# Building the identity tiles on VectorE instead of GpSimd, and taking two buffers of the last block together, in a linear-attention, PReLU and soft-MoE kernel

## The chip, the cores and the metric

The kernel runs on one core of a Trainium2 chip. The metric is the device time of one execution in microseconds (us), as the median of several runs; a profile of one further execution tells where the time goes.

## The reference, cut to what matters

```
q, k, v: 8 batches x 8 heads x 576 x 64; w_phi: 64 x 128
phi(x): p = x @ w_phi; p = p - max|p| over the features; [exp(p), exp(-p)]
kv = phi(k)^T v;  z = sum over s of phi(k)
x  = (phi(q) kv) / (phi(q) . z + 1e-6)              -> 4608 x 512
h  = x @ w_in;  g = max(h, 0) + alpha * min(h, 0);  x = g @ w_out
logits = x @ phi (32 slots);  d = softmax over tokens;  slot_in = d^T x
slot_out = max(slot_in @ w1[e], 0) @ w2[e]           (8 experts, 4 slots each)
out = softmax over slots of logits, @ slot_out       -> 4608 x 512
```

All inputs are float32.

## The kernel before

The 4608 tokens are cut into 12 blocks of 384 columns. For each block the kernel forms the query features and attends (`q_pair`, four head pairs), divides (`q_finish`), multiplies by `w_in` in 16 chunks of 128 rows (`gemm`, 12 matmuls each, into the tile `ph`), applies the PReLU (`leaky`, tile `gT`), and turns each chunk into the tile `gb` by 32x32 block transposes (`turn_g`). `softmax` then takes the logits of a block, and its `gather` (line 596, tile `pS`) sums `gb` weighted by the exponentials. The key side (`k_pair`) is done along the way. `w_in` and `w_out` come in as 32-bit words of another float format and are turned into float32 by a chain of VectorE and ScalarE operations (`conv`, lines 187 to 199).

The query features need the largest absolute value of the projection over all 128 partitions. That is GpSimd's `partition_all_reduce` (line 405: `pj` in, `mb` out), 48 times in the program. VectorE subtracts it (line 409), and ScalarE takes the exponentials (line 415). GpSimd also clears small tiles `zt` with memsets (line 347). Line 126 (`make_identity`) builds the 128x128 identity `ident` on GpSimd: a memset (masks.py:197) and an affine select (masks.py:199). `ident` serves TensorE's transposes, and from it `setup_b` adds up `tident`, four 32x32 identities side by side, repeated down the partitions.

The program is written as steps of a list ("slots", sixteen to a block), and a scheduler then orders the instructions of each engine. Each engine runs its own instructions strictly in that order; transfers are issued by SyncE's queue, also in order.

`gb` has three buffers of 8 chunks. A block takes one at its chunk 0 and a second at its chunk 8, and gives them back when its gather has read them. When the last block is reached, buffers that have become free are filled with the weights of the experts (`fetch`, line 702): two pieces of 256 KB into each `w` buffer whose chunk has been multiplied (line 745), and six pieces into a `gb` buffer at slot 186 (line 747). At the end the kernel multiplies the slots by `w1` (line 805, tile `pe`) and `w2` (line 823, `pso`), forms the output (line 859, `po`), and writes it (line 867).

Of the kernel before, what the change touches and what calls it, by code (L numbers as in the profile page):

```python
# [9 lines left out]
F32 = mybir.dt.float32  # L10
# [4 lines left out]
ALU = mybir.AluOpType  # L15
# [11 lines left out]
BT = 384  # L27
NB = T // BT
# [35 lines left out]
def attention_prelu_softmoe(ctx: ExitStack, tc, qT, kT, v, wphi, w_in, w_out, alpha, phi, w1, w2, out):  # L64
    nc = tc.nc
# [14 lines left out]
    pools = {}  # L80

    def open_pool(name, side=None):
        cm = tc.tile_pool(name=name, bufs=1, side=side) if side else tc.tile_pool(name=name, bufs=1)
        pools[name] = cm, cm.__enter__()
        return pools[name][1]

    def close_pool(name):
        pools.pop(name)[0].__exit__(None, None, None)
# [3 lines left out]
    def together(calls, before=None):  # L92
        held = before is not None
        for i, call in enumerate(calls):
            if i == 0:
                ins = call().ins
            else:
                with tc.high_priority():
                    ins = call().ins
            if i or held:  # L100
                tc.add_manual_dep(ins, before.name, nosync, reason="issued together")
            before = ins
        return before

    def spin(count, before, turn=None):
        turn = turn or bank("spin", ps_d)
        return together([
            lambda i=i: nc.tensor.matmul(turn[:, 128 * (i % 4):128 * (i % 4) + 128], ident, ident, start=True, stop=True)  # L108
            for i in range(count)], before)

    def bank(name, pool=None):
        if pool is not None:
            return pool.tile([128, 512], F32, tag={id(ps_h): "h", id(ps_l): "l", id(ps_d): "d"}[id(pool)], name=name)
        return ps_a.tile([128, 512], F32, tag="a", name=name)
# [6 lines left out]
    prep = open_pool("prep")  # L121
# [1 line left out]
    att = open_pool("attq", "right")  # L123

    ident = const.tile([128, 128], F32, name="ident")
    make_identity(nc, ident)
    wp = att.tile([128, F], F32, name="wp")
    nc.sync.dma_start(wp, wphi)
    alpha_sb = const.tile([128, NC], F32, name="alpha_sb")
# [3 lines left out]
    tident = const.tile([128, 128], F32, name="tident")  # L133
# [7 lines left out]
    cm = const.tile([128, NT], F32, name="cm")  # L141

    def setup_a():
        nc.vector.memset(ones, 1.0)

    def setup_b():
        nc.sync.dma_start(alpha_sb, alpha)
        nc.vector.tensor_scalar(out=alpha_neg, in0=alpha_sb, scalar1=-1.0, scalar2=None, op0=ALU.mult)
        nc.sync.dma_start(phi_sb, phi.rearrange("(k p) s -> p k s", p=128))
        for j in range(4):  # L150
            o = tident[:, 32 * j:32 * j + 32]
            nc.vector.tensor_tensor(out=o, in0=ident[:, 0:32], in1=ident[:, 32:64], op=ALU.add)
            nc.vector.tensor_tensor(out=o, in0=o, in1=ident[:, 64:96], op=ALU.add)
            nc.vector.tensor_tensor(out=o, in0=o, in1=ident[:, 96:128], op=ALU.add)

    sched = {}
    mark = {}
# [3 lines left out]
    def step_of(slot):  # L161
        return slot + VS * sum(slot > r for r in after)
# [320 lines left out]
    gb, pl_t, gT_t = {}, {}, {}  # L483

    def gemm(n, c):
        xhi, xlo = xhi_t[n], xlo_t[n]
        ph = ps_h.tile([128, 512], F32, tag="h", name="ph")
        h = ph[:, 0:BT]
        first = [(k, a, b) for k in range(KD) for a, b in ((0, 0), (1, 0))] + [(k, 0, 1) for k in range(KD)]
        terms = first if c == 0 else [(k, a, b) for k in range(KD) for a, b in ((0, 0), (0, 1), (1, 0))]  # L490
        for i, (k, a, b) in enumerate(terms):
            gemm_last[0] = nc.tensor.matmul(  # L492
                h, (w_in_hi, w_in_lo)[a][c][:, 128 * k:128 * k + 128], (xhi, xlo)[b][:, k, :],
                start=(i == 0), stop=(i == len(terms) - 1)).ins
        return h

    def leaky(n, c, h):
        gT = gT_t[n, c] = sm.tile([128, 512], F32, tag="gT", name="gT", bufs=5)[:, 0:BT]
        if n < NDEF or (c % 2 == 0 and n < NB - 1):
            nc.scalar.activation(gT, h, AF.Relu, scale=-1.0)  # L500
            nc.scalar.activation(h, h, AF.Relu)  # L501
            ins = nc.vector.scalar_tensor_tensor(out=gT, in0=gT, scalar=alpha_neg[:, c:c + 1], in1=h, op0=ALU.mult, op1=ALU.add).ins  # L502
        else:
            nc.vector.tensor_scalar(out=gT, in0=h, scalar1=0.0, scalar2=alpha_sb[:, c:c + 1], op0=ALU.min, op1=ALU.mult)  # L504
            ins = nc.vector.scalar_tensor_tensor(out=gT, in0=h, scalar=0.0, in1=gT, op0=ALU.max, op1=ALU.add).ins
        mark[NC * n + c] = ins
        if n < NDEF:
            nc.sync.dma_start(gT_d[n, c], gT)
# [11 lines left out]

    def turn_g(n, c):
        gT = gT_t[n, c]
        if c % 8 == 0:
            gb[n, c // 8] = pools["gp"][1].tile([128, 8, BT], F32, tag="gb", name="gb", bufs=3)
        nc.vector.transpose(out=gb[n, c // 8][:, c % 8, :], in_=gT)  # L525
        if c % 4 == 3:
            if c == 3:
                pl_t[n] = (bank("pl") if n < NDEF else bank("pl", ps_l))[:, 0:BT]
            before = None
            if (n, c) == (NB - 1, NC - 1):  # L530
                before = spin(SPIN[0], gemm_last[0])
            last = together([
                lambda g=g: nc.tensor.matmul(  # L533
                    pl_t[n][32 * g:32 * g + 32, :], wpr[:, c - 3 + g, :], gT_t.pop((n, c - 3 + g)), start=(c == 3), stop=(c == NC - 1))
                for g in (3, 2, 1, 0)], before)
            if before is not None:
                spun[0] = spin(SPIN[1], last)
# [137 lines left out]
    at(NC * (NB - 1) - 6, "post", lambda: combine(0, NT - 8))  # L675
    at(NC * (NB - 1) + 8, "post", lambda: combine(NT - 8, NT - 4))
    at(-44, "pre", setup_a)
    at(-42, "pre", setup_b)

    pieces = [("wo", c) for c in range(NC)]  # L680
# [25 lines left out]
    for step in range(-45, step_of(nslots + 4)):  # L706
        slot = real.get(step)
        for fn in sched.get((step, "pre"), ()):
            fn()
        h = None  # L710
        if slot is not None:
            n, c = divmod(slot, NC)
            if 0 <= slot < nslots:
                h = gemm(n, c)
            pn, pc = divmod(slot - 1, NC)
            if NDEF <= pn < NB:
                turn_g(pn, pc)
        for fn in sched.get((step, "virtual"), []) + sched.get((step, "pe"), []) + sched.get((step, "pe2"), []):
            fn()
        if h is not None:  # L720
            leaky(n, c, h)
        for fn in sched.get((step, "post"), ()):
            fn()
        if slot is None:
            continue
        if slot == NC * NDEF:
            close_pool("prep")
            open_pool("gp")
        if slot == 152:
            for tag in ("kraw", "khi", "klo", "vte", "vto", "kp1", "ks"):  # L730
                fetch(attk, tag)
            for i in range(3):
                fetch(attk, "vg", 1, 3)
            for i in range(KPB):
                fetch(attk, "kp2", 2, KPB)
        if slot == 168:
            close_pool("attq")
            pf = open_pool("pf", "right")
            for i in range(PF):
                fetch(pf, f"pf{i}")  # L740
        if slot == NC * (NB - 1):
            fetch(xp, "num", 3)
            fetch(xp, "bc", 3)
        if NC * (NB - 1) < slot <= nslots:
            fetch(wring, f"w{(slot - 1) % NC}", 2)
        if slot == 186:
            fetch(pools["gp"][1], "gb", 6, 3)
        if slot == nslots:
            fetch(xp, "xhi", 3)
            fetch(xp, "xlo", 3)  # L750
    gp = pools["gp"][1]
# [40 lines left out]
    for eg in range(2):  # L792
        for j in range(4):
            nc.vector.tensor_reduce(
                out=own[:, j:j + 1], in_=ident[:, 36 * j + 16 * eg:36 * j + 16 * eg + 4], axis=AX.X, op=ALU.add)
# [3 lines left out]
    for eg in range(2):  # L799
        hr = attk.tile([128, EF], F32, tag="kp2", name="hr", bufs=KPB)  # L800
        for fh in range(2):
            pe = ps_h.tile([128, 512], F32, tag="h", name="pe")
            for k in range(KD):
# [3 lines left out]
                out=hr[:, 512 * fh:512 * fh + 512], in0=pe, scalar1=0.0, scalar2=own[:, 4 + eg:5 + eg], op0=ALU.max, op1=ALU.min)  # L807
        t = acc[2 * eg:2 * eg + 2]
        for b in range(2):
            nc.vector.transpose(  # L810
                out=t[b].rearrange("p (b s) -> p b s", s=32),
                in_=hr.rearrange("p (f b) -> p b f", b=32)[:, 16 * b:16 * b + 16])
# [110 lines left out]
```

## Time and profile before

| | us |
|---|---|
| median of 3 runs (lowest to highest) | 1011.63 (1010.61 to 1012.14) |
| profiled execution, its own time | 1010.69 |
| its span | 1008.9 |
| TensorE matmuls busy | 949.4 |
| VectorE busy | 761.1 |
| ScalarE busy | 446.1 |
| GpSimd busy | 145.1 |

Busy time counts instructions that work; register, branch, semaphore and DMA-issuing instructions do not count. TensorE is busy 94% of the span as a whole, but not everywhere: the first 25 us hold 8.7 us of matmuls. In the rows the engines are PE (TensorE), PEld (its weight loads), DVE (VectorE), ACT (ScalarE), POOL (GpSimd) and SP (SyncE); a q behind the name is the engine's instruction queue. A row of a timeline has the start and the duration in us, and in brackets the idle time of the engine just before and what ended it.

### The profile page before, as it was taken

The page shows a single profiled execution, that of the slowest core. Times are in us where ns is not written, and L with a number is a line of the kernel's source. Part 1 is how long each engine was busy: PE and PEld are TensorE (multiplying, and loading weights), DVE is VectorE, ACT ScalarE, POOL GpSimd, SP SyncE. Part 2 cuts the span into 40 slices and gives each one's busy share as a digit, 9 for nine tenths or more (in the row PEclk, how much of TensorE's full clock was granted, in tenths as well). Part 3 has the DMA queues.
Part 4 walks back from the last instruction along what each step waited for, and adds up shares of the span by engine and source line. Part 5 has one row for each costly group of instructions (what it writes and reads, how often), then busy time and mean ns, then how long its engine had stood idle before and what let it go on. Part 6 is the DMA issues. An engine that isn't in the chain of part 4 may idle for free.

```text
span 1008.9 us, 22365 instructions
## 1 busy us (share of the span) xinstructions
PE 949.4 (94%) x9266; PEld 666.9 (66%) x9266; DVE 761.1 (75%) x1509; ACT 446.1 (44%) x883; POOL 145.1 (14%) x86
## 2 busy tenths in 40 slices
PE   3798897999999999999999999999999999999997
PEld 1455675677757777666677677676677677887554
DVE  2998996999697778868878678768977568787134
ACT  2876874777553434435225435335225343200113
POOL 2200121220211211112102212112003140000000
PEclk9898997999999999999999999999999999999999
DMA  6345664556231120021321031031414011469999
GB/s 208 110 151 159 205 191 107 186 174 206 60 91 33 28 81 27 22 78 53 89 92 53 27 81 40 9 86 50 125 34 139 13 48 44 170 201 309 335 351 340
DMA packets 75685, 121.26 MB, mean 120 GB/s; under 512 B 7872, under 2 KB 49472, under 8 KB 75584
## 3 DMA queue, kind: packets, MB, share of 16 engines
q1 hardware_dynamic: 75584, 119.84, 38.6%
q8 instruction: 73, 1.20, 0.5%
q14 instruction: 28, 0.23, 0.1%
HBM read 98.71 MB, written 21.10 MB: 119 GB/s over the span
## 4 chain that ended last, share of the span: by engine, by line
PE 68%; DVE 6%; DMA 1%; ACT 1%; issue 1%; SPq 0%; DVEq 0%; ACTq 0%
PE ph L492 34%; PE num L425 5%; PE pkv L323 5%; PE pS L596 4%; PE pl L533 3%; PE pq L393 3%; PE den L431 3%; PE pk L279 2%; PE pso L823 2%; PE pe L805 1%; PE po L859 1%; PE idle L108 1%; DVE gb L525 1%; PE pr L551 1%; PE pt L345 1%; PE spin L108 1%
## 5 line engine op out<-in xcount | busy, mean ns | idle before, releaser
L492 PE MATMUL ph<-xhi,w 128*128 128x384 f32 x1536 | 434.1, 351 | 14.3 <-ACT xhi L465 7.0
L492 PEld LDWEIGHTS ph<-xhi,w 128*128 128x128 f32 x1536 | 279.4, 189 | 82.8 <-issue 41.5
L492 PE MATMUL ph<-xlo,w 128*128 128x384 f32 x768 | 256.3, 341 | 0.0
L405 POOL PARTITION_ALL_REDUCE mb<-pj x48 | 138.5, 2887 | 524.2 <-ACT pj L399 427.5
L492 PEld LDWEIGHTS ph<-xlo,w 128*128 128x128 f32 x768 | 143.8, 188 | 9.8 <-issue 5.7
L500 ACT ACTIVATE gT<-ph 128x384 f32<-128x384 f32 x104 | 50.7, 487 | 163.8 <-PE ph L492 139.9
L525 DVE STREAM_TRANSPOSE gb<-gT 128x384 f32<-128x384 f32 x192 | 106.0, 566 | 4.6 <-DMA gT<-gT_d 2.1
L504 DVE TENSOR_SCALAR gT<-ph,alpha_sb 128x384 f32<-128x384 f32 x88 | 53.6, 610 | 60.5 <-PE ph L492 60.2
L502 DVE SCALAR_TENSOR_TENSOR gT<-gT,alpha_neg,ph 128x384 f32<-128x384 f32 x104 | 63.0, 606 | 47.7 <-ACT ph L501 46.7
L415 ACT ACTIVATE qe<-pj 128x768 f32<-128x768 f32 x92 | 74.1, 839 | 41.5 <-DVE pj L409 27.9
L323 PE MATMUL pkv<-kp,vt 128*64 128x256 f32 (+1 forms) x640 | 86.8, 406 | 0.7 <-ACT kp L274 0.7
L425 PE MATMUL num<-qe,kv 128*64 128x192 f32 (+1 forms) x496 | 72.9, 413 | 2.6 <-ACT qe L415 2.1
L273 ACT ACTIVATE kp<-kp 128x512 f32<-128x512 f32 (+1 forms) x80 | 46.7, 585 | 64.0 <-DVE kp L272 63.5
L323 PEld LDWEIGHTS pkv<-kp,vt 128*64 128x64 f32 (+1 forms) x640 | 42.1, 142 | 38.2 <-issue 18.3
L596 PE MATMUL pS<-gb,d 32*32 32x256 f32 x2304 | 55.0, 385 | 1.2 <-issue 1.2
L270 DVE TENSOR_REDUCE mx<-pk 128x4 f32<-128x512 f32 (+1 forms) x80 | 50.1, 627 | 4.7 <-PE pk L279 3.3
L393 PE MATMUL pq<-qraw,wp 64*128 64x384 f32 x192 | 49.0, 560 | 5.0 <-DMA qraw<-in_qT_dram 3.9
L409 DVE TENSOR_TENSOR pj<-pj,mb 128x768 f32<-128x768 f32 x48 | 46.7, 974 | 8.2 <-POOL mb L405 8.1
L279 PE MATMUL pk<-wp,kraw 64*128 64x128 f32 x512 | 39.7, 298 | 14.0 <-issue 10.0
L272 DVE TENSOR_TENSOR kp<-pk,mx 128x512 f32<-128x512 f32 (+1 forms) x80 | 50.4, 629 | 2.3 <-PE pkv L323 1.7
L425 PEld LDWEIGHTS num<-qe,kv 128*64 128x64 f32 x496 | 31.8, 136 | 28.9 <-issue 18.1
L501 ACT ACTIVATE ph<-ph 128x384 f32<-128x384 f32 x104 | 50.6, 487 | 0.0
(196 smaller groups left out, 1211.5 us busy)
## 6 DMA issues: line engine op xcount, KB each, us to landing
w<-in_w_dram SPq DMA_DIRECT2D x46, 256.0 KB
qraw<-in_qT_dram SPq DMA_DIRECT2D x48, 192.0 KB
bc<-rc_d SPq DMA_DIRECT2D x24, 384.0 KB
out_dram<-os SPq DMA_DIRECT2D x18, 512.0 KB
raw<-in_w_in_dram SPq DMA_DIRECT2D x16, 512.0 KB
raw<-in_w_out_dram SPq DMA_DIRECT2D x16, 512.0 KB
pf<-in_w_dram SPq DMA_DIRECT2D x26, 256.0 KB
gT_d<-gT SPq DMA_DIRECT2D x32, 192.0 KB
```

The lines of the kernel that those rows point to most:

```text
L279: lambda t=t, j=j, sl=slice(64 * j, 64 * j + 64): nc.tensor.matmul(st["pk"][:, j, F * t:F * t + F], st["kraw"][sl, 128 * t:128 * t + 128], ...
L323: return lambda: nc.tensor.matmul(pkv[64 * j:64 * j + 64, 0:256], vt[:, 64 * j:64 * j + 64], feats(t, j).rearrange("p s f -> p (s f)"), st ...
L393: lambda j=j, sl=slice(64 * j, 64 * j + 64): nc.tensor.matmul(pq[j][:, 0:BT], wp[sl], st["qraw"][sl], start=True, stop=True)
L405: nc.gpsimd.partition_all_reduce(mb, pj, 128, bass_isa.ReduceOp.absmax)
L415: nc.scalar.activation(st["e", s], pj, AF.Exp, scale=(1.0, -1.0)[s])
L425: lambda s=s, j=j: nc.tensor.matmul(num[64 * j:64 * j + 64, o:o + w], kvs[:, s, 64 * j:64 * j + 64], st["e", s][:, j, o:o + w], start=(s = ...
L492: gemm_last[0] = nc.tensor.matmul(h, (w_in_hi, w_in_lo)[a][c][:, 128 * k:128 * k + 128], (xhi, xlo)[b][:, k, :], start=(i == 0), stop=(i = ...
L500: nc.scalar.activation(gT, h, AF.Relu, scale=-1.0)
L502: ins = nc.vector.scalar_tensor_tensor(out=gT, in0=gT, scalar=alpha_neg[:, c:c + 1], in1=h, op0=ALU.mult, op1=ALU.add).ins
L504: nc.vector.tensor_scalar(out=gT, in0=h, scalar1=0.0, scalar2=alpha_sb[:, c:c + 1], op0=ALU.min, op1=ALU.mult)
L525: nc.vector.transpose(out=gb[n, c // 8][:, c % 8, :], in_=gT)
L596: lambda j=j, i=i, h=h: nc.tensor.matmul(pS[i][32 * (j % 4):32 * (j % 4) + 32, 256 * h:256 * h + 256], st["d"][32 * i:32 * i + 32, 32 * j: ...
```

## The change

`make_identity` goes, and `setup_a` builds both tiles on VectorE: a row number in each 32-column tile by doubling (`col`), its block transpose (`row`), four comparisons of the two into `tident`, a memset of `ident`, and four copies of 32x32 blocks from `tident` to the diagonal of `ident`. The twelve additions of `setup_b` go. In `turn_g` the last block takes both its `gb` buffers at its chunk 0, and the fetch into the third `gb` buffer moves from slot 186 to slot 181.

```diff
     ident = const.tile([128, 128], F32, name="ident")
-    make_identity(nc, ident)
     wp = att.tile([128, F], F32, name="wp")
...
     def setup_a():
+        col = prep.tile([128, 32], F32, name="col")
+        row = prep.tile([128, 32], F32, name="row")
+        nc.vector.memset(col[:, 0:1], 0.0)
+        for w in (1, 2, 4, 8, 16):
+            nc.vector.tensor_scalar(out=col[:, w:2 * w], in0=col[:, 0:w], scalar1=float(w), scalar2=None, op0=ALU.add)
+        nc.vector.transpose(out=row, in_=col)
+        nc.vector.memset(ident, 0.0)
+        for j in range(4):
+            sl = slice(32 * j, 32 * j + 32)
+            nc.vector.tensor_tensor(out=tident[:, sl], in0=col, in1=row, op=ALU.is_equal)
+            nc.vector.tensor_copy(ident[sl, sl], tident[sl, sl])
         nc.vector.memset(ones, 1.0)
...
     def setup_b():
...
-        for j in range(4):
-            o = tident[:, 32 * j:32 * j + 32]
-            nc.vector.tensor_tensor(out=o, in0=ident[:, 0:32], in1=ident[:, 32:64], op=ALU.add)
-            nc.vector.tensor_tensor(out=o, in0=o, in1=ident[:, 64:96], op=ALU.add)
-            nc.vector.tensor_tensor(out=o, in0=o, in1=ident[:, 96:128], op=ALU.add)
...
     def turn_g(n, c):
         gT = gT_t[n, c]
-        if c % 8 == 0:
-            gb[n, c // 8] = pools["gp"][1].tile([128, 8, BT], F32, tag="gb", name="gb", bufs=3)
+        for h in (c // 8,) if n < NB - 1 else range(2):
+            if c % 8 == 0 and (n, h) not in gb:
+                gb[n, h] = pools["gp"][1].tile([128, 8, BT], F32, tag="gb", name="gb", bufs=3)
...
-        if slot == 186:
+        if slot == 181:
             fetch(pools["gp"][1], "gb", 6, 3)
```

In the changed kernel line numbers are 5 to 6 higher, so that its L352 and L410 are the L347 and L405 of before. The engines' orders differ at the start (GpSimd and VectorE) and in the last block (SyncE's queue); GpSimd's and SyncE's are shown. On ScalarE nothing moves, and on TensorE only which of two buffers of weights comes first at line 805.

GpSimd's first instructions before (an ISA row without a tile is the instruction that sets GpSimd's code for the next one; the last row is the first `partition_all_reduce`):

```order
masks.py:197 MEMSET ident 128x128
L347 MEMSET zt 128x128 x3
masks.py:199 ISA
masks.py:199 AFFINE_SELECT ident<-ident 128x128
L347 MEMSET zt 128x128 x5
L405 ISA
L405 ISA mb<-pj 128x768
```

and GpSimd's first instructions in the changed kernel:

```order
L915 MEMSET const-bfloat16-1.0 128x1
L915 MEMSET const-uint8-127 128x1
L924 UNCONDITIONAL_BRANCH
L352 MEMSET zt 128x128 x8
L410 ISA
L410 ISA mb<-pj 128x768
```

The memset and the select of `ident` are gone, one of the two code-setting instructions is gone with them, and the eight `zt` memsets stand together ahead of the one that is left.

SyncE's queue in the last block before, where weights are fetched into freed buffers (each `w` row is one chunk's buffer, in the order of the chunks from 0; rows of one kind are left out at both ends):

```order
L702 DMA w_9690<-in_w_dram 128x512 x2
L702 DMA w_9715<-in_w_dram 128x512 x2
L702 DMA w_9735<-in_w_dram 128x512 x2
L702 DMA w_9755<-in_w_dram 128x512 x2
L702 DMA w_9775<-in_w_dram 128x512 x2
L702 DMA w_9808<-in_w_dram 128x512 x2
L702 DMA w_9829<-in_w_dram 128x512 x2
L702 DMA gb<-in_w_dram 128x512 x3
L702 DMA w_9849<-in_w_dram 128x512 x2
L702 DMA gb<-in_w_dram 128x512 x3
L702 DMA w_9876<-in_w_dram 128x512 x2
```

and the same place of the same queue in the changed kernel:

```order
L708 DMA w_9693<-in_w_dram 128x512 x2
L708 DMA w_9718<-in_w_dram 128x512 x2
L708 DMA gb<-in_w_dram 128x512 x6
L708 DMA w_9738<-in_w_dram 128x512 x2
L708 DMA w_9765<-in_w_dram 128x512 x2
L708 DMA w_9785<-in_w_dram 128x512 x2
```

The six `gb` pieces stood behind nine and ten chunks' buffers; now all six stand behind four, ahead of the buffers of chunks 4 to 15.

## Rows read from the trace of the kernel before

**Rows 1.** The page, part 2: VectorE busy in tenths, 40 slices of 25.2 us.

```profile
DVE  2998996999697778868878678768977568787134
```

**Rows 2.** Timeline of GpSimd in the first 20 us.

```profile
0.87 0.49 POOL L347 MEMSET zt<- 128x128 f32 x3
9.36 0.28 POOL masks.py:199 TENSOR_SCALAR_AFFINE_SELECT ident<-ident 128x128 f32<-128x128 f32 x1 [8.00 <-issue]
9.61 0.77 POOL L347 MEMSET zt<- 128x128 f32 x5
19.05 2.75 POOL L405 PARTITION_ALL_REDUCE mb<-pj  x1 [8.67 <-issue]
```

**Rows 3.** Instructions of masks.py:199 and L405: duration min/median/max in ns, first to last start.

```profile
masks.py:199 POOLq MODIFY_POOL_CONFIG  x2: 11/11/11, 1.4 to 1.4; - x2
...
L405 POOLq MODIFY_POOL_CONFIG  x2: 1/1/1, 10.6 to 10.6; - x2
```

**Rows 4.** Timeline of VectorE, 8 to 28 us.

```profile
9.68 0.50 DVE L152 TENSOR_TENSOR tident<-ident 128x32 f32<-128x32 f32 x4 [8.78 <-POOL ident masks.py:199]
...
13.03 0.69 DVE L272 TENSOR_TENSOR kp<-pk,mx 128x512 f32<-128x512 f32 x1
21.84 2.46 DVE L409 TENSOR_TENSOR pj<-pj,mb 128x768 f32<-128x768 f32 x1 [8.12 <-POOL mb L405]
24.22 0.61 DVE L189 TENSOR_SCALAR m<-m 128x512 f32<-128x512 f32 x1
...
27.60 0.95 DVE L409 TENSOR_TENSOR pj<-pj,mb 128x768 f32<-128x768 f32 x1
```

**Rows 5.** Timeline of ScalarE, the first 30 us.

```profile
5.58 0.86 ACT L397 COPY pj<-pq 128x384 f32<-128x384 f32 x2 [3.57 <-PE pq L393]
...
14.66 0.67 ACT L187 ACTIVATE m<-raw 128x512 f32<-128x512 f32 x1
```

**Rows 6.** Timeline of TensorE, the first 30 us.

```profile
6.84 2.08 PE L279 MATMUL pk<-wp,kraw 64*128 64x128 f32 x16 [1.26 <-DMA kraw<-in_kT_dram]
```

**Rows 7.** Timeline of the end: dependent small VectorE operations.

```profile
927.43 0.21 DVE L570 TENSOR_SCALAR nm<-mbl,mrun 128x1 f32<-128x1 f32 x1
927.68 0.16 DVE L571 TENSOR_TENSOR sc<-mrun,nm 128x1 f32<-128x1 f32 x1
```

**Rows 8.** VectorE's groups by shape: the smallest full-height block transpose.

```profile
L673 DVE STREAM_TRANSPOSE logits<-cw 128x128 f32<-128x128 f32 x2 | 0.6, 288 | 0.0
```

**Rows 9.** Windows of 2 us: length, busy by engine, TensorE clock, DMA share, GB/s.

```profile
18.00:20.00 2.00, 0.00 (x0) 0.00 (x0) 0.00 (x0) 0.00 (x0) 0.95 (x1) 1.00 0.01 4
...
40.00:42.00 2.00, 0.27 (x2) 0.30 (x3) 1.97 (x5) 1.58 (x4) 1.13 (x1) 0.50 0.24 33
```

**Rows 10.** Windows, the stretch behind the start.

```profile
24.00:50.00 26.00, 18.67 (x185) 10.56 (x185) 25.25 (x45) 22.32 (x40) 6.85 (x3) 0.87 0.34 101
```

**Rows 11.** VectorE's waits from 24 to 200 us: total us, times, longest.

```profile
DVE num L472 <- DMA bc<-rc_d: 9.1, 2, 6.0
```

**Rows 12.** The chain of waits, 800 us to the end: the gather of block 10.

```profile
890.86 3.94 PE pS L596 x170
```

**Rows 13.** Timeline of SyncE's queue in the last block and behind it.

```profile
884.76 22.73 SPq L702 DMA_DIRECT2D w<-in_w_dram  x18
907.54 1.37 SPq L702 DMA_DIRECT2D gb<-in_w_dram  x3
...
927.81 3.08 SPq L702 DMA_DIRECT2D gT<-in_w_dram  x5
...
934.63 7.55 SPq L702 DMA_DIRECT2D gb<-in_w_dram  x12
```

**Rows 14.** Windows of 5 us in the last block and behind it.

```profile
895.00:900.00 5.00, 5.00 (x32) 4.12 (x32) 4.18 (x7) 0.00 (x0) 0.00 (x0) 1.00 0.35 105
...
925.00:930.00 5.00, 3.59 (x28) 2.99 (x24) 2.88 (x14) 1.24 (x4) 0.00 (x0) 1.00 0.91 275
...
935.00:940.00 5.00, 3.98 (x98) 2.93 (x80) 1.29 (x2) 1.17 (x2) 0.00 (x0) 1.00 0.98 312
```

## The prediction

> **What bounds the kernel now.** I read the page's slices first. TensorE sets most of the span, but the start is a stage of its own: VectorE is at 2 tenths in the first 25 us and at 9 in the two slices behind it [rows 1]. So from 24 us on VectorE sets the pace for a while (25.25 us busy out of 26 [rows 10]), and what counts is when that stretch may begin.
>
> The timeline of VectorE says what it waits for: it has nothing to do from 13.72 us (13.03 + 0.69) to 21.84, when the first result `mb` of GpSimd arrives, 8.12 us later [rows 4]. The timeline of GpSimd says why `mb` is late. Its input `pj` has been ready since 6.44 us (5.58 + 0.86 [rows 5]), yet the first partition_all_reduce starts at 19.05. Ahead of it GpSimd idles twice, 8.00 us before the affine select of `ident` and 8.67 us before the reduce, and neither wait is for another engine ("issue") [rows 2]. Each gap begins with a MODIFY_POOL_CONFIG, at 1.4 and at 10.6 us, one for the select and one for the reduce [rows 3]. The 47 later reduces have no such instruction. I read the two gaps as GpSimd fetching the code of an operation that it did not hold, 8.0 us (9.36 - 1.4) and 8.45 us (19.05 - 10.6). They run one behind the other, and all of the kernel stands behind the second.
>
> At the other end I read SyncE's queue, the windows and the chain of waits in the last block.
>
> **The change part by part.**
>
> *GpSimd at the start.* The memset and select of `ident` go, and with them the first code fetch. The five `zt` memsets that stood behind the select (0.77 us [rows 2]) now stand ahead of the only fetch, which took its start at 1.4; with them it would begin at 2.2, and somewhat less for the memset of `ident`, which goes. I take 2.05 us. The price of that fetch is bounded by the two rows of its kind: 7.96 us gives a first reduce at 10.0, 8.45 us gives 10.5. I take 8.45, for it is the same operation's. The first reduce then starts 8.55 us earlier than 19.05. A third bound is further down.
>
> *VectorE's additions.* One memset, five additions and one transpose depend on each other in turn; a memset of `ident`, four comparisons and four copies follow. Dependent small operations start 0.25 us apart [rows 7]; a 128x128 transpose takes 0.288 us [rows 8], and this one is a quarter of that. So 7 x 0.25 + 0.3 and nine more at 0.11 to 0.25 each, about 3 to 4.3 us from 0.8 us on. They end by 5.1 us, on an engine that did nothing then but wait 8.78 us for `ident` [rows 4]. Its first real work, the reduce of `pk` (line 270), needs the projection, ready at 8.92 us [rows 6]. The additions cost nothing; if that cover were gone, all of them would cost at most 4.3 us. The twelve additions that go took 1.3 us and stood in the path of `pk`: the four operations on `pk` that ended at 13.72 now begin at 8.95 instead of 10.98 and end near 11.7.
>
> *What is late next.* The first reduce takes 2.75 us, 10.5 to 13.25, and VectorE is free by 11.7. So the subtraction at line 409 starts at 13.3 instead of 21.84, 8.5 us earlier. It would again take 2.46 us beside the second reduce (0.95 us when none runs [rows 4]); the projections for that one are copied in the 2 us that VectorE gives back. Behind it stands line 189, at 24.22 before. It needs the first of the raw weights through ScalarE: line 187 ran at 14.66 + 0.67 [rows 5], and if that is held by the landing of the transfer and cannot move, line 189 can start at 15.33 at the earliest. That is the third bound: a gain of 8.9 us at most. With 8.5 it starts at 15.7, so the transfer does not bind. The other first loads are no limit either: the DMA engines are idle again from 18 us on (share 0.01 [rows 9]), and the next loads are issued when VectorE has read a buffer, so they move along.
>
> *From there to the end.* No engine waits for a point in time. Each engine's order is the same as before, VectorE's stretch begins 8.5 us earlier, and the buffers come free and the loads are issued as much earlier. The stalls further on, such as the 9.1 us that VectorE waits for the broadcast `bc` [rows 11], hang on loads that move along, so I let them stand at their size. The gain of 8.5 us goes through.
>
> *The last block.* The `gb` pieces now stand behind the `w` buffers of chunks 0 to 3. They wait for the gather of block 10, which ends at 894.80 [rows 12]; the buffers of chunks 4 and up wait for matmuls behind that same gather, so nothing that could have started is held up: at most the six issues, at 1.37 / 3 us each [rows 13], 2.7 us, in a window where the DMA engines are busy 0.35 of the time [rows 14]. These 1.5 MB then no longer move at 908 to 914. Does that help the end? From 935 us the DMA engines are full (0.98 and above [rows 14]), but what they then carry is issued only when the buffers `gT` and `gb` come free, at 927.81 and 934.63 [rows 13], and just before, at 925 to 930, they have a little room (0.91). So the room made earlier can't be used later. Bounds: no gain, or the 9% of that 5 us window, 0.45 us. I take 0. A loss is excluded up to the slack of SyncE's queue, which the rival below treats.
>
> *Sum.* 8.5 us off the profiled execution's 1010.69: 1002.2. That execution stands 0.9 us below the median of the runs, 1011.63, from which the same sum gives 1003.1. I predict the middle, **1002.7 us**.
>
> *A page beside it.* By the Trainium skill, GPSIMD Engine Reference, section Instruction dispatch, the first call of a freshly loaded GpSimd kernel pays some 6 us for loading its code, without a profile instruction. The trace agrees on the kind and shows more: 7.96 and 8.45 us. If only 6 us went, the sum would be 1004.7, inside the range below. The sum goes by the trace.
>
> **The rivals.**
>
> *The fetch isn't what holds the reduce* (or the change leaves it as late). The second gap ends at 19.05, about 1 us after the DMA engines drain at 18 us [rows 9]; if the reduce's code comes only when the first loads are through, it starts near 19 whatever stands ahead of it. For it: the two times lie close. Against it: the first gap ended at 9.36 in the midst of those loads and was of nearly the same length. Gain 0 to 1 us: 1009.7 to 1010.7, or up to 1011.6 from the median. Chance 0.06.
>
> *Part is given back further on.* The start moves, but a stall behind it grows: the broadcast `bc` shares the DMA queue with the raw loads, and if these come more densely the 9.1 us [rows 11] may grow; or the TensorE clock, at half (1.2 GHz) at 40 to 42 us after matmuls had stood still [rows 9], falls in one more stretch. One such stretch of 6 us under full work costs about 3 us, one half again of that stall 4.5 us. For it: both occur here. Against it: the program's order and its gaps stay. 1005 to 1007. Chance 0.09.
>
> *The fetch of `gb` blocks SyncE's queue (slower).* Place: behind chunk 3's buffer in the last block. If the buffer that the fetch takes were one that the last block itself fills, its wait would end only with the last gather, when the next `gb` issues start, at 934.63 [rows 13], and the 24 pieces of chunks 4 to 15, six of `xhi` and `xlo` and its own six would all wait there: 36 x 0.26 MB = 9.4 MB, at 312 GB/s [rows 14] 30 us of transfers put behind that time, where the DMA engines are full. 1002.7 + 30 = 1033. It decides from the point where the wait lasts more than some 8.5 us beyond what the weights have to spare. Against it: block 10 holds two of the three buffers, the last block takes the third and then the first, so the second is left, free at 894.80. Chance 0.02; other ways to be slower 0.01.
>
> **How the numbers follow.** The forecast, with all of the front gain going through: 0.82, and its times reach from 1001 (gain of 9 with 0.45 at the end, from the profiled time) to 1005 (6 us, or a part lost). The range goes from 1000.6 to 1006.2: at the lower end it leaves an execution's scatter below, at the upper end it takes in half of the second rival; it holds some 0.8. About 0.2% (2 us) is what a measurement of this kernel can tell from no change. Faster than that: 0.82 + 0.09 + 0.01 of the first rival = 0.92. Within it: 0.05, the rest of that rival. Slower: 0.03.
>
> **What would show it.** Right: one MODIFY_POOL_CONFIG pair, near 2 us; the first reduce at 10 to 10.6; line 409 (there 414) at about 13.3; VectorE's first slice at 5 or 6 tenths instead of 2; the last gather and the first output issue each 8 to 9 us earlier; six `gb` issues at 885 to 890 in one piece. Wrong: a first reduce at 18 or later; a gap of VectorE of several us behind 15 us, or a `bc` wait much above 9 us; an idle TensorE at line 805.

## The result, and the profile after

| | us |
|---|---|
| before, median of 4 runs on this chip (lowest to highest) | 1011.86 (1010.61 to 1012.14) |
| changed kernel, median of 4 runs | 1000.85 (999.73 to 1002.52) |
| ratio, 95% interval | 0.9902 (0.9889 to 0.9915) |
| changed kernel, profiled execution (its span) | 1001.29 (999.5) |

The change takes 1.0% off: between the two profiled executions 9.4 us (1010.69 to 1001.29), between the medians 11.0. The time is in the range, 1.85 us below the predicted 1002.7. The way there was not quite the one predicted.

The page, part 2, VectorE's slices (25 us each), and the instructions of line 410, the `partition_all_reduce` (duration in ns, then first and last start):

```profile
DVE  6999987999687688767978588767977567786234
```

```profile
L410 POOLq MODIFY_POOL_CONFIG  x2: 6/6/6, 2.0 to 2.0; - x2
```

VectorE's first slice has risen from 2 to 6 tenths [rows 1], and of the two places with a MODIFY_POOL_CONFIG [rows 3] one is left, at 2.0 us. The timeline of GpSimd, the first 21 us, against [rows 2]:

```profile
0.73 1.24 POOL L352 MEMSET zt<- 128x128 f32 x8 [0.29 <-POOLq L915]
6.66 2.74 POOL L410 PARTITION_ALL_REDUCE mb<-pj  x1 [4.69 <-ACT pj L402]
12.38 2.81 POOL L410 PARTITION_ALL_REDUCE mb<-pj  x1 [2.97 <-ACT pj L402]
19.91 2.74 POOL L410 PARTITION_ALL_REDUCE mb<-pj  x1 [4.72 <-ACT pj L402]
```

Both gaps marked "issue" are gone, not one of them. The instruction that sets the code is still there, but no gap marked "issue" follows it: the reduce starts at 6.66 us, as soon as its input `pj` is there, 12.39 us earlier than at 19.05. I had let it start at 10.5. (This trace alone leaves room for a fetch of up to 4.7 us, hidden under the wait for `pj`; `early_reduce` below tests that.)

The gain is smaller than those 12.4 us, and the timelines of ScalarE and of VectorE say why. ScalarE, against [rows 5]:

```profile
5.71 0.86 ACT L402 COPY pj<-pq 128x384 f32<-128x384 f32 x2 [3.70 <-PE pq L398]
...
14.44 0.66 ACT L192 ACTIVATE m<-raw 128x512 f32<-128x512 f32 x1 [1.62 <-DMA raw<-in_w_in_dram]
```

VectorE, against [rows 4]:

```profile
2.90 0.78 DVE L153 COPY ident<-tident 32x32 f32<-32x32 f32 x4
...
11.04 0.69 DVE L277 TENSOR_TENSOR kp<-pk,mx 128x512 f32<-128x512 f32 x1
11.64 0.95 DVE L414 TENSOR_TENSOR pj<-pj,mb 128x768 f32<-128x768 f32 x1
15.14 0.43 DVE L194 TENSOR_SCALAR m<-m 128x512 f32<-128x512 f32 x1 [2.55 <-ACT m L192]
...
18.69 0.95 DVE L414 TENSOR_TENSOR pj<-pj,mb 128x768 f32<-128x768 f32 x1
```

The new identity ends at 3.68 us (2.90 + 0.78), on an engine that would have been idle. Line 414 starts right behind the work on `pk`, with no wait for `mb`. Then VectorE waits 2.55 us for line 192 on ScalarE, and ScalarE itself waits 1.62 us for the raw weights to land. That is a new wait: before, neither engine waited here. Line 194 starts at 15.14 (24.22 before): 9.1 us earlier. The second line 414 starts at 18.69 (27.60): 8.9 earlier. The third reduce starts at 19.91 (28.70): 8.8 earlier.

From there on the shift can be read from the starts of the reduces, the n-th in each kernel (timeline of GpSimd). The two rightmost columns are distances, the 4th to the 5th reduce and the 9th to the 10th:

| kernel | 4th | 5th | 9th | 10th | 4th to 5th | 9th to 10th |
|---|---|---|---|---|---|---|
| before | 37.57 | 99.40 | 154.78 | 180.55 | 61.83 | 25.77 |
| before with the new `gb` part (`gb_only`) | 37.12 | 100.15 | 155.53 | 180.15 | 63.03 | 24.62 |
| changed kernel | 28.79 | 91.09 | 146.50 | 170.90 | 62.30 | 24.40 |
| changed kernel, old `gb` part (`ident_only`) | 28.49 | 90.76 | 146.16 | 171.54 | 62.27 | 25.38 |
| changed kernel, second profile (`again`) | 28.48 | 90.59 | 145.96 | 170.54 | 62.11 | 24.58 |

At the 4th reduce the two profiled executions stand 8.78 us apart, and this is what the start gains. (Over all the profiles below whose order behind the start is unchanged, the 4th reduce stands at 28.2 to 29.1 us with the new start and at 37.1 to 38.4 with the old.) Behind it the distance is 8.3 us at the 9th and 9.65 at the 10th, and 9.4 at the end of the span. These later steps of about 1 us do not come from the start, and whether the `gb` part has a share in them is open. The distance from the 9th to the 10th reduce goes with the `gb` part: it is 25.38 to 25.77 us in the three profiles with the old part (`reduce_first`, below, has 25.48) and 24.18 to 24.92 in seven with the new one. The 4th to the 5th tends the other way (61.83 to 62.27 with the old part, 61.48 to 63.06 with the new), and the medians of `gb_only` and `ident_only` below show no share. No run shows how a part that changes the last block could act here. The stretch between the 9th and the 10th holds the wait for `bc` and, behind it, a stretch at the lower TensorE clock (0.50 is 1.2 GHz). The windows of 5 us behind that wait, of before and then of the changed kernel, with the granted clock third from the end:

```profile
160.00:165.00 5.00, 0.00 (x0) 0.00 (x0) 0.67 (x2) 0.08 (x1) 0.00 (x0) 0.65 0.82 221
165.00:170.00 5.00, 4.51 (x21) 3.70 (x22) 5.00 (x11) 3.30 (x8) 0.00 (x0) 0.50 0.15 40
170.00:175.00 5.00, 5.00 (x32) 3.76 (x34) 4.88 (x13) 4.86 (x9) 0.00 (x0) 0.83 0.27 68
```

```profile
152.00:157.00 5.00, 0.31 (x1) 0.31 (x2) 1.46 (x4) 0.87 (x2) 0.00 (x0) 0.72 0.74 200
157.00:162.00 5.00, 5.00 (x27) 4.18 (x27) 5.00 (x12) 3.30 (x8) 0.00 (x0) 0.60 0.21 52
162.00:167.00 5.00, 5.00 (x43) 3.18 (x41) 4.89 (x13) 4.97 (x10) 0.20 (x1) 1.00 0.19 46
```

Before, TensorE works again from about 165.5 us and the clock is back at about 171.7; in the changed kernel the two times are 156.7 and 161.0. (These are estimates from the busy time and the mean clock of the windows, with a clock of either 0.50 or 1.00.) So 6.2 us of work at the lower clock stand against 4.3. At half the clock the 1.9 us between them are worth some 0.9 us, most of the 1.4 by which the two distances differ. The wait for `bc` itself is nearly the same, 8.4 us against 9.1 [rows 11]:

```profile
DVE num L477 <- DMA bc<-rc_d: 8.4, 2, 5.5
```

At the end, the chain of waits has the gather of block 10 at 880.66 (890.86 [rows 12]), 10.2 us earlier:

```profile
880.66 3.95 PE pS L602 x172
```

and the timeline of SyncE's queue has the six `gb` issues in one piece, from 882.75 to 886.49 (885 to 890 forecast), and the first output at 968.60 (977.92 before), 9.3 us earlier. For both, 8 to 9 us were forecast. The rows of the changed kernel, then the row of before:

```profile
882.75 3.74 SPq L708 DMA_DIRECT2D gb<-in_w_dram  x6
...
968.60 1.29 SPq L873 DMA_DIRECT2D out_dram<-os  x2
```

```profile
977.92 26.05 SPq L867 DMA_DIRECT2D out_dram<-os  x18
```

### The profile page after: what moved, and what is told of

The parts are those of the page before. It is cut to its first block, busy times and chain, and to the rows that moved or that the text cites. A ratio compares the mean times of both kernels' runs of the same rounds, so it can differ in the third digit from the quotient of the medians.

```text
span 999.5 us, 22367 instructions
## 1 busy us (share of the span) xinstructions
PE 946.8 (95%) x9266; PEld 665.6 (67%) x9266; DVE 761.0 (76%) x1513; ACT 445.8 (45%) x883; POOL 142.9 (14%) x84
## 4 chain that ended last, share of the span: by engine, by line
PE 70%; DVE 6%; issue 1%; ACT 1%; DVEq 0%; ACTq 0%
PE ph L497 35%; PE pkv L328 5%; PE num L430 5%; PE pS L602 4%; PE pl L539 3%; PE pq L398 3%; PE den L436 3%; PE pk L284 2%; PE pso L829 2%; PE pe L811 1%; PE po L865 1%; PE idle L108 1%; DVE gb L531 1%; PE pr L557 1%; PE pt L350 1%
## 5 line engine op out<-in xcount | busy, mean ns | idle before, releaser
L410 POOL PARTITION_ALL_REDUCE mb<-pj x48 | 136.7, 2848 | 526.2 <-ACT pj L404 430.0
L278 ACT ACTIVATE kp<-kp 128x512 f32<-128x512 f32 (+1 forms) x80 | 46.7, 585 | 62.0 <-DVE kp L277 61.6
L510 DVE SCALAR_TENSOR_TENSOR gT<-ph,gT 128x384 f32<-128x384 f32 x88 | 48.6, 552 | 1.8
L279 ACT ACTIVATE kp<-kp 128x512 f32<-128x512 f32 (+1 forms) x80 | 46.7, 585 | 1.3
```

The costliest lines, as they stand in the source:

```text
L410: nc.gpsimd.partition_all_reduce(mb, pj, 128, bass_isa.ReduceOp.absmax)
```

## The experiments

The runs are to tell four things: which part of the change gains; whether the gain is the identity on VectorE or the missing switch of GpSimd's code; why no switch is left; and whether the landing of the raw weights is what ends last now. Times are medians in us.

**Each part alone.** `ident_only` is the changed kernel with the part in the last block undone:

```diff
-        for h in (c // 8,) if n < NB - 1 else range(2):
-            if c % 8 == 0 and (n, h) not in gb:
-                gb[n, h] = pools["gp"][1].tile([128, 8, BT], F32, tag="gb", name="gb", bufs=3)
+        if c % 8 == 0:
+            gb[n, c // 8] = pools["gp"][1].tile([128, 8, BT], F32, tag="gb", name="gb", bufs=3)
...
-        if slot == 181:
+        if slot == 186:
```

> The identity on VectorE alone, the last block's buffers and fetch as before. Theory (the whole gain is made at the start; moving six weight pieces earlier leads into room that cannot be used): 1000.5 to 1002, a ratio of 0.989 to 0.991 to the kernel before, the same as with both parts. Rival (the earlier fetch has a share in the 11 us, which is more than the 8.5 that were forecast for the start): 1002.5 to 1004.

`gb_only` is the kernel before with the same lines changed the other way.

> Both buffers at once and the earlier fetch alone, the identity on GpSimd as before. Theory: no change, 1011 to 1012.5. Rival (the fetch gives a share): 1009 to 1010.5.

Measured: `ident_only` 1001.63, ratio 0.9914 (0.9901 to 0.9928); `gb_only` 1010.3, ratio 1.0000 (0.9991 to 1.0009). The start has the whole gain, and the part in the last block is worth nothing that can be measured, in either company; the interval of `gb_only` leaves room for 0.9 us either way. As a bonus `gb_only` shows the old start once more. Its timeline of GpSimd:

```profile
8.62 0.28 POOL masks.py:199 TENSOR_SCALAR_AFFINE_SELECT ident<-ident 128x128 f32<-128x128 f32 x1 [7.26 <-issue]
...
18.61 5.50 POOL L405 PARTITION_ALL_REDUCE mb<-pj  x2 [8.97 <-issue]
```

The two gaps are 7.26 and 8.97 us here, 8.00 and 8.67 before [rows 2]: they vary by up to 0.7 us from one execution to the next.

**The switch without the identity.** `select_back` is the changed kernel with the affine select put back, into a tile that nobody reads. Nothing waits for it but GpSimd:

```diff
     ident = const.tile([128, 128], F32, name="ident")
+    spare = prep.tile([128, 128], F32, name="spare")
+    make_identity(nc, spare)
```

> The changed kernel plus the memset and affine select on GpSimd, into a spare tile that nobody reads: VectorE waits for no identity, yet GpSimd has to switch code twice. Theory (the switch is the loss): the first reduce is back at 18.5 to 19.5 us and the time at 1009.5 to 1012. Rival (the wait of VectorE for the identity, 8.8 us, was the loss): the time stays at 1000 to 1003.

Measured: 1011.67, ratio to before 1.0006 (0.9993 to 1.0018). The whole gain is gone. The timeline of GpSimd, the instructions of line 412 (the reduce), and the timeline of VectorE:

```profile
9.54 0.28 POOL masks.py:199 TENSOR_SCALAR_AFFINE_SELECT spare<-spare 128x128 f32<-128x128 f32 x1 [8.18 <-issue]
9.79 0.77 POOL L354 MEMSET zt<- 128x128 f32 x5
19.89 5.50 POOL L412 PARTITION_ALL_REDUCE mb<-pj  x2 [9.32 <-issue]
```

```profile
L412 POOLq MODIFY_POOL_CONFIG  x2: 1/1/1, 10.8 to 10.8; - x2
```

```profile
22.67 2.46 DVE L416 TENSOR_TENSOR pj<-pj,mb 128x768 f32<-128x768 f32 x1 [11.19 <-POOL mb L412]
```

Where `ident` comes from does not decide; that GpSimd runs a select ahead of its first reduce costs all of the gain. The two gaps, 8.18 and 9.32 us, are back as a pair.

**A reduce ahead of everything.** If the first reduce of the program has to fetch code, a small reduce at the very start does that early. `early_reduce` is the changed kernel with one on a tile of ones that nobody reads:

```diff
+    spare = prep.tile([128, 32], F32, name="spare")
+    spare2 = prep.tile([128, 32], F32, name="spare2")
+    nc.vector.memset(spare, 1.0)
+    nc.gpsimd.partition_all_reduce(spare2, spare, 128, bass_isa.ReduceOp.absmax)
```

> The changed kernel plus a reduce of a small tile of ones as early as GpSimd can: it starts when the code is there and so measures the fetch by itself, which in the changed kernel only shows as at most 4.7 us, since the reduce then waited for its input. Theory (the reduce's code is there quickly when no other code was called before): the small reduce starts 1 to 4.7 us behind its code-setting instruction, the first real reduce at 6.6 us as in the changed kernel, and the time does not move, 1000 to 1002.5, since the wait that ends last is that of the first raw weights at 14.4 us. Rival (a fetch always takes 8 us, and in the changed kernel it ran before the span): the small reduce starts with no gap at all.

Measured: 1002.13, ratio 0.9921 (0.9906 to 0.9936), as the changed kernel. Its timeline of GpSimd:

```profile
1.49 0.44 POOL L129 PARTITION_ALL_REDUCE spare<-spare  x1
...
6.84 2.74 POOL L414 PARTITION_ALL_REDUCE mb<-pj  x1 [4.33 <-ACT pj L406]
```

The small reduce runs at 1.49 us with no gap ahead of it. That is the rival's sign; the 1 to 4.7 us of the theory did not come. So within the execution no fetch is hidden ahead of 6.66 us: GpSimd already has the reduce's code when the program begins. How the code got there this run cannot say; `iota_last` below bears on it.

**The same small reduce in the kernel before.** `reduce_first` keeps the identity on GpSimd, and the old `gb` part, and only puts the small reduce ahead of the select (its memset and select are written out, so that they stand behind it):

```diff
-    make_identity(nc, ident)
+    spare = prep.tile([128, 32], F32, name="spare")
...
+    nc.gpsimd.partition_all_reduce(spare2, spare, 128, bass_isa.ReduceOp.absmax)
+    nc.gpsimd.memset(ident, 0.0)
+    sel = nc.gpsimd.affine_select(
+        out=ident, in_=ident, compare_op=ALU.not_equal, fill=1.0, base=0, pattern=[[-1, 128]], channel_multiplier=1)
```

> The kernel before, with its identity on GpSimd, plus one reduce of a small tile of ones ahead of the affine select. Theory (GpSimd holds the reduce's code when the program starts, and that code also has the affine select, so that only the order in which the two are first called makes it switch): one code-setting instruction, no gap behind it, the select at about 2 us, the first real reduce at 6.6 us, and the whole gain without VectorE: 1000.5 to 1002.5. Rival (the affine select itself needs its own code, whatever ran before): a gap of 7 to 9 us ahead of the select or of the next reduce, 1009 to 1012.

Measured: 1001.65, ratio to before 0.9908 (0.9892 to 0.9924). This is all of the gain, with the identity still on GpSimd. Timeline of GpSimd, and the instructions of line 129:

```profile
1.35 0.43 POOL L129 PARTITION_ALL_REDUCE spare<-spare  x1
1.68 0.36 POOL L131 TENSOR_SCALAR_AFFINE_SELECT ident<-ident 128x128 f32<-128x128 f32 x1
...
6.64 2.74 POOL L411 PARTITION_ALL_REDUCE mb<-pj  x1 [3.73 <-ACT pj L403]
```

```profile
L129 POOLq MODIFY_POOL_CONFIG  x2: 11/11/11, 1.2 to 1.3; - x2
```

The only MODIFY_POOL_CONFIG is the small reduce's. The select has none and starts right behind it: the code that serves the reduce serves the select as well. In the kernel before the select came first, other code was set for it, and the reduce had to have its own set again.

**What is on GpSimd when the program starts.** `iota_last` is the changed kernel with one more GpSimd operation near the end, which needs other code and leaves it behind; its output is read by nobody:

```diff
+    spare = sm.tile([128, 1], I32, tag="rs", name="spare", bufs=2)
+    nc.gpsimd.iota(spare, pattern=[[0, 1]], base=0, channel_multiplier=1)
```

> The changed kernel plus an iota on GpSimd at the very end, long after the last reduce, which sets the other code; nobody reads its result. Theory A (the reduce's code is at hand at the start because the execution before left it there): with the other code left behind, the first reduce starts 8 to 8.7 us behind its code-setting instruction, at 10 to 10.7 us instead of 6.7; since VectorE has 2.5 us to spare up to the first raw weights, the end moves by 1 us at most, 1000.5 to 1002.5. Theory B (something ahead of the program sets it): the first reduce stays at 6.6 us.

Measured: 1002.12, ratio 0.9914 (0.9900 to 0.9929). The timeline of GpSimd at the start, the instructions of the added line, and the timeline of VectorE:

```profile
9.31 2.75 POOL L410 PARTITION_ALL_REDUCE mb<-pj  x1 [7.36 <-issue]
```

```profile
L822 POOLq MODIFY_POOL_CONFIG  x2: 88/88/88, 821.6 to 821.6; - x2
```

```profile
12.10 0.96 DVE L414 TENSOR_TENSOR pj<-pj,mb 128x768 f32<-128x768 f32 x1 [0.31 <-POOL mb L410]
15.07 0.86 DVE L194 TENSOR_SCALAR m<-m 128x512 f32<-128x512 f32 x1 [2.02 <-ACT m L192]
```

The code is set for the iota at 821.6 us, behind the last reduce (818.88); the iota itself runs at 880.89:

```profile
880.89 0.14 POOL L822 IOTA spare<- 128x1 int32 x1 [59.27 <-DVE lsum L586]
```

This operation gives the first reduce, which stands ahead of it in the program, a gap of 7.36 us, a little less than the 8 to 8.7 expected. The plain reading is that it does so from one execution to the next: what an execution uses last is what the next one finds. (That something sets the code anew at each start isn't excluded by a run, but it would have to choose what the program uses last.) And the 2.65 us by which the first reduce is now later (9.31 against 6.66) cost nothing: line 194 starts at 15.07 as before, with VectorE still waiting 2.02 us for ScalarE. The start has slack between `mb` and the raw weights.

**Taking away the new wait.** Is the landing of the raw weights what ends last? The first raw transfer is issued earlier in SyncE's queue. `raw_early` moves it further up (slot -43, shown) than `raw_early2` (slot -38); in both the first `Abs` (line 192) is tied to its place behind an exponential of the key side:

```diff
-            nc.scalar.activation(m, high, AF.Abs)
+            ins = nc.scalar.activation(m, high, AF.Abs).ins
+            if slot == -16:
+                tc.add_manual_dep(ins, held[1].name, nosync, reason="where it stood")
...
-        at(slot - 2, "pre", load)
+        at(-43 if slot == -16 else slot - 2, "pre", load)
```

> The changed kernel with the load of the first raw weights issued five places earlier, behind the first three projections' inputs. Theory (behind the reduce, the landing of these 0.5 MB at 14.4 us is what VectorE waits for): line 194 starts at 13 to 14 us instead of 15.14, and the time falls by 1 to 2 us, to 999 to 1000, so far as the scheduler's new order of the later instructions allows. Rival (the next limit is right behind it, in ScalarE's order or in the other loads, which now land later): line 194 not earlier than 14.5, the time at 1000.5 or above.

> The same with the load only two places earlier, ahead of the last two value tiles: it should land about 1.6 us earlier than in the changed kernel, line 194 near 13.5 to 14.2 us, 999.5 to 1000.5. Rival as there: 1000.5 or above.

Measured: 1009.77, ratio 0.9986 (0.9974 to 0.9998), and 1003.4, ratio 0.9919 (0.9904 to 0.9934). Neither answers the question, for the edit moved more than a transfer: the scheduler put ScalarE's `Sign`, which reads the same weights, ahead of the work on `pj` and `kp`, and there it waits. The timeline of ScalarE in `raw_early` and in `raw_early2`:

```profile
9.68 0.66 ACT L196 ACTIVATE sign<-raw 128x512 f32<-128x512 f32 x1 [3.16 <-DMA raw<-in_w_in_dram]
```

```profile
13.91 0.66 ACT L196 ACTIVATE sign<-raw 128x512 f32<-128x512 f32 x1 [3.40 <-DMA raw<-in_w_in_dram]
```

In `raw_early` the 4th reduce is even earlier (27.48), and the time is lost behind it (5th reduce 95.22 against 91.09, last 825.26 against 817.87). In which steps it is lost I did not follow up.

`raw_kept` (slot -41) also ties `Sign` to its place behind `Abs`, so that every engine other than SyncE has the order of the changed kernel; `again` is the changed kernel once more, beside it.

```diff
+            ins2 = nc.scalar.activation(sign, high, AF.Sign).ins
+            if slot == -16:
+                tc.add_manual_dep(ins2, ins.name, nosync, reason="where it stood")
...
+        at(-41 if slot == -16 else slot - 2, "pre", load)
```

> The changed kernel with the first raw weights loaded right behind the first value tile, and with the first Abs and Sign on ScalarE held where they stood, so that every engine's order stays that of the changed kernel and only this one load moves. Theory (their landing is what ends last behind the first reduce): ScalarE takes Abs right behind its exponential, at 12.8 us instead of 14.44, line 194 starts near 13.5 us instead of 15.14, and the time falls by 1.2 to 1.7 us against the changed kernel. Rival (the other loads, which now land later, or the stalls further on take it back): 0 to 0.7 us.

> The changed kernel once more, as the measure for the run beside it: 1000 to 1002.5 us.

Measured: `raw_kept` 1001.22, ratio 0.9892 (0.9874 to 0.9909); `again` 1001.49, ratio 0.9898 (0.9883 to 0.9913). No difference. The timelines of ScalarE in `raw_kept`, and in `again`:

```profile
12.81 0.65 ACT L193 ACTIVATE m<-raw 128x512 f32<-128x512 f32 x1
...
16.56 0.68 ACT L193 ACTIVATE m<-raw 128x512 f32<-128x512 f32 x1 [0.92 <-DMA raw<-in_w_in_dram]
```

```profile
14.11 0.66 ACT L192 ACTIVATE m<-raw 128x512 f32<-128x512 f32 x1 [1.28 <-DMA raw<-in_w_in_dram]
...
16.86 0.67 ACT L192 ACTIVATE m<-raw 128x512 f32<-128x512 f32 x1
```

The first `Abs` no longer waits and runs 1.3 us earlier. But the second piece of raw weights is now what ScalarE waits for, and of the 1.3 us only 0.3 are left at the second `Abs`, and as many at the third reduce (19.29 against 19.60). So ScalarE waits for the landing of the first raw weights in the changed kernel, and for the second piece when the first comes earlier. To bring one piece forward alone gains nothing in the time, as the rival had it. Whether bringing both forward would gain was not run.

## Why the prediction was right, and where its steps were not

- *GpSimd's gaps hold the start.* Right: `select_back` puts them back and the gain is gone, `reduce_first` takes them away in another manner and has all of it. The rival that the fetch isn't what holds the reduce falls with this.
- *The price of the one fetch that stays, 8.45 us from 2.05.* This step failed. I read each gap as an operation fetching code that GpSimd did not hold, so I took one away and kept one. The two gaps had one cause: the select displaced the reduce's code, and the reduce had it set back. With the select gone neither is paid, and the first reduce starts at 6.66, not 10.5, held only by `pj`. `early_reduce` and `iota_last` show it: no gap ahead of an even earlier reduce, and a gap of 7.36 us once a call of other code stands behind the last reduce.
- *VectorE's additions cost nothing.* Right: from 0.81 to 3.68 us, 2.9 us of elapsed time against the 3 to 4.3 forecast, and the first work on `pk` stands at 8.99 (8.95 forecast).
- *Line 409 (414) at 13.3, 2.46 us long.* Both numbers failed. It starts at 11.64, right behind the work on `pk`, since `mb` is there by 9.40, and it takes 0.95 us, since the second reduce does not begin until 12.38. The 2.46 us stand where a reduce is under way from its start on (before, `select_back`).
- *The third bound, "the transfer does not bind".* This failed too, and as a consequence. With the reduce at 6.66 the bound that I had worked out (line 189 no earlier than 15.33, a gain of at most 8.9) decides when line 194 starts: 15.14, a gain of 9.08. `raw_kept`, where the weights land earlier, has that line at 13.50. Of the 12.4 us that the reduce moved, some 2.2 are lost because VectorE is still at work on `pk`; 1.5 come back because line 414 is shorter; and 2.55 go into the wait for ScalarE, of which 1.62 is the landing.
- *The size came out by luck, in good part.* By my own sum line 194 would have started at 15.7, with a fetch that was not there and no wait for the weights. The missing fetch put the reduce 3.8 us earlier, and the work on `pk` and the weights took back all but 0.6.
- *The gain goes through, and the stalls keep their size.* Right within the scatter: 8.8 us at the 4th reduce, 8.3 at the 9th, 9.65 at the 10th, 9.4 at the end of the span, against 8.5. `bc` went from 9.1 to 8.4. The sign of the second rival did come, one more stretch at the lower TensorE clock, at 14 to 21 us (last section), but it cost no more than some tenths of a microsecond: `ident_only` does not have it, and its 4th reduce stands at 28.49 against 28.79.
- *The last block, 0.* Right, shown from both sides by `gb_only` and `ident_only`. The six issues stand in one piece.
- *The sum.* 8.5 us were forecast off the profiled 1010.69, and 9.4 came: 0.3 more by the start (8.8 at the 4th reduce), the rest behind it, where steps of about 1 us come and go and a share of the `gb` part is not excluded. That the medians lie 11.0 apart is the widest of the comparisons: in the other sessions before's medians are 1010.79 to 1011.48, and the kernels with an early first reduce and the order otherwise unchanged stand 8.7 to 10.3 below them.
- *The page.* The Trainium skill, GPSIMD Engine Reference, section Instruction dispatch, names some 6 us for a first call of freshly loaded code. The gaps here are 7.26 to 9.32 us, so the trace stays above it. The time that I worked out from it, 1004.7, took the 6 us off the profiled execution alone; off the middle that the forecast goes by it would be 1005.2. Neither came, since no such load was left.

## What to carry to other kernels

In this kernel, idle time of GpSimd that ends in "issue" behind a MODIFY_POOL_CONFIG went with a change of its code, and a MODIFY_POOL_CONFIG with the code already there had no gap behind it. Before moving the odd operation to another engine, look at which operation GpSimd calls first: here a select ahead of the first reduce cost two changes, and a reduce of 0.43 us ahead of the select saves both, with 1001.65 us as good as the rewritten identity. When two such gaps stand in a row, don't count them as two independent prices, and when a gap goes, work out the next bound for the case that it goes entirely. A bound that only just does not bind deserves a second number.

## What was not expected of the hardware

- GpSimd's code seems to stay from one execution to the next: an iota behind the last reduce of the program gave the first reduce a gap of 7.36 us, and without it there is none. What executed just before each profile is not on record, so this stays a reading.
- One setting of the code served both the reduce and the affine select when the reduce came first (`reduce_first`); when the select came first, the reduce needed another. Why the select alone gets other code is open.
- The gaps: 7.26, 8.00 and 8.18 us ahead of a select, 7.36 ahead of the reduce in `iota_last`, 8.67, 8.97 and 9.32 ahead of the reduce behind a select.
- TensorE's clock at the start does not go with the way the kernel starts. In the changed kernel TensorE stands still at 14 to 16 us and is granted 0.50 (1.2 GHz) behind it; before, it stood still longer, 16.8 to 24.8, and the windows show 1.00 there and behind. But `ident_only`, with the new start, shows 1.00 too, and `select_back`, with the old one, shows 0.50. Windows of 2 us of the changed kernel, then of 4 us of the kernel before, then of 2 us of `ident_only` and of `select_back`:

```profile
14.00:16.00 2.00, 0.00 (x0) 0.00 (x0) 0.86 (x3) 1.56 (x3) 1.19 (x1) 0.56 1.02 407
16.00:18.00 2.00, 1.34 (x12) 1.37 (x14) 1.71 (x5) 2.00 (x5) 0.00 (x0) 0.50 0.67 246
18.00:20.00 2.00, 2.00 (x12) 0.92 (x11) 1.61 (x3) 2.00 (x5) 0.09 (x1) 0.50 0.63 168
```

```profile
16.80:20.80 4.00, 0.00 (x0) 0.00 (x0) 0.00 (x0) 0.00 (x0) 1.75 (x1) 1.00 0.22 79
20.80:24.80 4.00, 0.00 (x0) 0.00 (x0) 2.96 (x3) 0.47 (x1) 3.75 (x2) 1.00 0.00 0
24.80:28.80 4.00, 2.87 (x18) 2.20 (x18) 3.68 (x9) 4.00 (x9) 0.10 (x1) 1.00 0.20 42
```

```profile
16.00:18.00 2.00, 1.64 (x15) 1.67 (x17) 1.70 (x4) 2.00 (x5) 0.00 (x0) 1.00 0.68 248
```

```profile
16.00:18.00 2.00, 0.00 (x0) 0.00 (x0) 0.00 (x0) 0.00 (x0) 0.00 (x0) 0.50 0.61 224
```

From line 194 to the third reduce the changed kernel's gain falls by 0.3 us (9.1 to 8.8). What decides in which executions the clock falls here no run shows.
